# A fused retention and token-mixing kernel: q in rows of four tokens, one eviction for two products, other tiles for pairs 2 and 3, and a new order of all steps

## The chip, the cores and the metric

The kernel runs on one core of one Trainium2 chip. The metric is the device time of one execution in microseconds, on that core. PE is the matrix engine, DVE, ACT and POOL are the three engines that work on vectors, SP issues most of the transfers between HBM (DRAM) and SBUF; sixteen DMA engines carry them out.

## What is computed

The reference computes two layers one after the other, for 4 batches, 8 heads, 768 tokens and 64 values a head:

```python
for t in range(S):                       # layer 1, for each batch and head
    state = gamma * state + outer(k[t], v[t])
    y[t] = scale * q[t] @ state
x = y.transpose(0, 2, 1, 3).reshape(B, S, 512)
wq, wk = x @ w_q, x @ w_k                # layer 2: 512 -> 64 each
mixed = (scale2 * wq @ wk.T) @ x         # over the 768 tokens of a batch
out = relu(mixed) @ w_out                # 512 -> 512
```

gamma differs by head. q, k, v and the output are float32, 6.3 MB each.

## The kernel before, in words

The 768 tokens of a batch are cut into three *pairs* of two chunks of 128 tokens, twelve pairs in all (pair p is batch p // 3). The recurrence is done by chunks: within a chunk through a masked 128x128 product of k and q (scores), between chunks through the 64x64 state that PE accumulates in PSUM over the whole batch. The decay is split: v is multiplied by gamma to the power of minus t when it is cast (fv), y by gamma to the power of t when it is evicted (fy). The second layer uses that (wq wk^T) x = wq (wk^T x): PE accumulates z = wk^T x over a batch, and then multiplies wq by z, so nothing of the second layer behind z can start before a batch's last pair has its x.

Each pair passes through the same steps. Names of steps and tiles, with the lines of the profile:

- load (L151): q_st, k_st and v_st of 512 KB each, float32, two neighbouring tokens to a partition, so that the DRAM side is read in pieces of 512 B. Weights: L166 and L171.
- ck, cq, cv: cast to bf16 into ks, qs, vs (L136 on ACT, L137 on DVE and POOL; cv multiplies, L362 and L556).
- trk, trq: transposes on PE (L386, L585, L605); ekq, ek, eq evict them into kq (L136, L137).
- sc: scores (L417, L627); eat: mask and eviction into at_sb (DVE, L429, L639).
- st: state (L496, L678); es: its eviction into s_sb.
- in, ic, ia: the parts of y from the state (L461, L481, L664) and from the scores (L517, L698); ex: eviction with decay into x_nat (L530, L712).
- xt, exT: transpose of x (L730) and its eviction into xT; wqk: x @ w_k, and wq transposed (L749, L758); ew and ewt: their evictions into wk_n and wqT, two instructions.
- zm, ez: z and its eviction (L790); mx: wq times z (L809); r: relu (L824, L826); pj: the projection with w_out (L831), two of 512 columns for each pair; eo: eviction into o_st (L844, by L136 or L137).
- store (L860): 512 KB for a pair, or 256 KB for one half (s11/1).

TYPES says for each pair how its chunks lie: in type "2" a chunk lies on 64 partitions with two tokens each, and the matmuls on it are 64 rows deep; in type "1" the casts bring a chunk onto all 128 partitions (four casts of 64 x 512 for k, and four for v, in place of one of 128 x 1024), and scores, inner products and state take half as many matmuls.

The order of everything is written out by hand (or by a search done beforehand): ORDER is a list of steps with the engine (A, V, P) and the PSUM bank (@n), and each engine executes its steps in that order. fill.n are n matmuls on a zero tile whose result nobody reads. LOADS is the order on SP's queue: first all loads, then the stores s0, s1 and so on. SP takes one after the other: whatever waits holds up all that is behind it. STAGES = 18 staging buffers of 512 KB are reused as casts free them; OBUFS = 11 output buffers are reused as stores read them. The store's access pattern and the load's are these:

```python
dst = out[b, cp*2*C : (cp+1)*2*C, :].rearrange("(g j) m -> g j m", j=2)     # L856: 128 x 2 x 512
nc.sync.dma_start(out=dst, in_=src, max_dma_last_dim=OBYTES)                 # L860
```

Of the kernel before, what the change touches and what calls it, by code (L numbers as in the profile page):

```python
# [9 lines left out]
FP32 = mybir.dt.float32  # L10
# [6 lines left out]
ck.0.0:V ck.0.1:A fill.15@6 trk.0@0 cq.0.1:A cq.0.0:V fill.4@6 trq.0@0 cv.0.1:P cv.0.0:V ekq.0.1:A  # L17
ekq.0.0:A ck.1:A fill.6@6 st.0.0 cq.1:V cv.1:P cv.2:P es.0.0:A sc.0.1@0 cv.3:P eat.0.1:V mask:P
ck.4.0:P ck.2:A ck.4.1:P fill.2@6 st.0.1 cv.4.0:P sc.0.0@2 trq.1@4 cv.4.1:P trk.1@4 WO.1:P
ekq.1.1:V ekq.1.0:V es.0.1:V cq.2:A ck.5.0:P fill.1@6 ia.0.1@0 WO.0:P in.0@0 fill.2@6 sc.1.0@4  # L20
eat.0.0:V fill.4@6 sc.1.1@2 st.1.0 eat.1.0:V es.1.0:A ia.0.0@0 cv.5.0:P trk.2@4 ic.0@0 trq.2@4
st.1.1 eat.1.1:V ekq.2.0:V W:A cv.5.1:P ekq.2.1:A ex.0:V fill.3@6 sc.2.0@4 sc.2.1@2 in.1@0
eat.2.0:V ia.1.1@0 ia.1.0@0 es.1.1:A ck.6.1:P xt.0@4 st.2.0 cv.6.1:P eat.2.1:V ic.1@0 exT.0:V
ia.2.1@2 ex.1:V ia.2.0@2 ck.3:A es.2.0:A trk.3@4 ic.2@2 in.2@2 ex.2:V cv.6.0:P cv.7.0:P cq.3:A
wqk.0@6 trq.3@4 ekq.3.1:A ekq.3.0:V xt.1@0 st.3.0 exT.1:V es.3.0:A xt.2@2 cq.4:A exT.2:V cv.7.1:P
sc.3.0@4 ew.0:V sc.3.1@0 wqk.1@2 wqk.2@3 eat.3.1:V ewt.1:A ew.1:A trq.4@0 eat.3.0:V trk.4@0
ck.8.0:P ewt.2:A ew.2:A st.3.1 ic.3@2 cq.8:P cv.8.0:P cv.8.1:P in.3@2 ia.3.0@2 ia.3.1@2 ek.4:V
zm.0.0@4 ewt.0:V eq.4:A es.3.1:A ex.3:V cv.9.1:P sc.4.0@0 sc.4.1@5 st.4.0 eat.4.0:V xt.3@2 exT.3:V
eat.4.1:V es.4.0:A zm.0.1@4 ez.0:A mx.0@0 ck.5.1:A cq.5:V in.4.1@2 cv.9.0:P wqk.3@4 r.0:A ewt.3:A
ew.3:A ia.4.0@2 ia.4.1@2 in.4.0@2 trk.5@5 mx.1@0 ex.4:V st.4.1 trq.5@5 ek.5:V r.1:A eq.5:V  # L30
ck.10.1:P pj.0.1@4 eo.0.1:A pj.0.0@0 sc.5.0@5 es.4.1:V xt.4@3 sc.5.1@1 cv.10.0:P st.5.0 eo.0.0:A
pj.1.0@0 eat.5.0:V ck.6.0:A eat.5.1:V pj.1.1@5 exT.4:A es.5.0:V ia.5.0@3 ia.5.1@3 in.5.1@3
in.5.0@3 eo.1.0:A mx.2@0 eo.1.1:A ck.11.1:P cq.6:V ex.5:V wqk.4@2 ew.4:V trq.6@5 trk.6@5 eq.6:V
r.2:A xt.5@0 ek.6:V ewt.4:A pj.2.1@3 pj.2.0@2 sc.6.0@5 ck.7.1:A exT.5:V sc.6.1@0 wqk.5@4 eo.2.1:A
zm.1.0@3 cq.7:V eat.6.0:V ew.5:V eat.6.1:V st.6.0 zm.1.1@3 eo.2.0:A ck.7.0:A trk.7@5 es.6.0:A
trq.7@5 ez.1:A st.6.1 ewt.5:A eq.7:V ek.7:V mx.3@2 ia.6.1@0 ia.6.0@0 es.6.1:A st.7.0 r.3:A
in.6.1@0 es.7.0:A ex.6:V sc.7.0@5 mx.4@2 pj.3.1@4 r.4:A sc.7.1@0 eat.7.0:V pj.3.0@2 st.7.1 xt.6@5
eat.7.1:V exT.6:V ck.8.1:A eo.3.1:A pj.4.0@3 eo.3.0:A ia.7.1@1 es.7.1:A trq.8@5 cq.11:P in.7.0@1
ck.9.1:V trk.8@5 eo.4.0:A mx.5@3 in.7.1@1 eq.8:V ck.9.0:A ia.7.0@1 pj.4.1@0 r.5:A eo.4.1:A ek.8:V
sc.8.0@5 sc.8.1@3 cq.9:A st.8.0 ex.7:V es.8.0:A xt.7@1 exT.7:A pj.5.0@0 eat.8.1:V trq.9@3 trk.9@3  # L40
in.8.1@1 eo.5.0:A eat.8.0:V ek.9:V eq.9:A cv.10.1:P in.8.0@1 ia.8.1@1 cv.11.0:P ia.8.0@1 pj.5.1@0
ex.8:V wqk.6@6 xt.8@1 ew.6:V eo.5.1:A sc.9.1@3 cq.10:A exT.8:V wqk.7@0 wqk.8@1 ew.7:A zm.2.0@2
ck.10.0:A eat.9.1:V sc.9.0@3 ew.8:V ewt.6:A zm.2.1@2 st.9.0 ewt.8:A ez.2:A trk.10@5 trq.10@5
mx.6@1 eat.9.0:V es.9.0:A st.9.1 ewt.7:A in.9.1@3 r.6:A ek.10:V ia.9.0@3 ia.9.1@3 mx.7@0 eq.10:V
es.9.1:A ex.9:V ck.11.0:A r.7:A sc.10.0@5 eat.10.0:V st.10.0 pj.6.0@2 trk.11@3 trq.11@3 eq.11:V
ek.11:V eo.6.0:A sc.10.1@0 es.10.0:A xt.9@5 eat.10.1:V pj.6.1@2 in.10.0@3 cv.11.1:P in.10.1@3
exT.9:A sc.11.0@5 eo.6.1:A st.10.1 es.10.1:A eat.11.0:V wqk.9@2 ia.10.1@3 ia.10.0@3 ew.9:A ewt.9:A
sc.11.1@0 ex.10:V mx.8@5 eat.11.1:V st.11.0 r.8:A pj.7.1@2 in.11.0@3 xt.10@5 exT.10:V es.11.0:A
in.11.1@3 ia.11.0@3 ia.11.1@3 pj.8.0@0 ex.11:V wqk.10@1 eo.7.1:A xt.11@3 ewt.10:V exT.11:V ew.10:A
eo.8.0:A pj.7.0@6 wqk.11@3 ew.11:V eo.7.0:A zm.3.0@0 ewt.11:V zm.3.1@0 ez.3:A mx.11@0 r.11:A  # L50
mx.10@3 mx.9@5 pj.8.1@2 pj.11.1@0 eo.8.1:A pj.11.0@1 eo.11.1:A r.10:V r.9:A pj.10.0@2 pj.10.1@0
eo.10.0:A eo.11.0:V eo.10.1:A pj.9.1@6 eo.9.1:A pj.9.0@2 eo.9.0:A
# [4 lines left out]
q0 v0 k1 q1 v1 k2 q2 w v2 k3 q3 v3 k4 q4 v4 o0 o1 k5 q5 v5 k6 q6 v6 k7 q7 v7 k8 q8 v8 k9 q9 v9 k10  # L57
q10 v10 k11 q11 v11 s0 s1 s2 s3 s4 s5 s6 s7 s8 s11/1 s11/0 s10/0 s10/1 s9/1 s9/0
""".split()

TYPES = "222211111111"
STAGES = 18
OBUFS = 11
# [7 lines left out]
def kernel(  # L71
# [38 lines left out]
    stage_pool = pool("stage", STAGES)  # L110
# [33 lines left out]
    def load(name, p, half=None, eng=None):  # L144
        src = {"k": k, "q": q, "v": v}[name]
        b, cp = divmod(p, NP)
        st = pairs[p]
        if name + "_st" not in st:
            st[name + "_st"] = stage_pool.tile([128, 2, HP, 2, D], FP32, name=name + "_st", tag="st")
        xs = slice(0, 2) if half is None else slice(half, half + 1)  # L150
        dma = (eng or nc.sync).dma_start(  # L151
            out=st[name + "_st"][:, xs].rearrange("g x hp j d -> g (x hp) (j d)"),
            in_=src[b, xs.start * HP : xs.stop * HP, cp * 2 * C : (cp + 1) * 2 * C, :].rearrange(
                "h (g j) d -> g h (j d)", j=2
            ),
        )
    wstages = {}

    def load_weights(token):
        w_st = stage_pool.tile([128, 2, HP, 2, D], FP32, name=token + "_st", tag="st").rearrange(  # L160
            "p x hp j d -> p (x hp j d)"
        )
        if token == "w":
            st = w_st[:, 0 : 2 * NDM * DH].rearrange("p (w a h) -> p w a h", w=2, a=NDM)
            for i, src in enumerate((moe_w_q, moe_w_k)):
                nc.sync.dma_start(out=st[:, i], in_=src.rearrange("(a p) h -> p a h", p=128))  # L166
        else:
            st = w_st.rearrange("p (a m) -> p a m", a=2)
            for i in range(2):
                a = 2 * int(token[1:]) + i  # L170
                nc.sync.dma_start(  # L171
                    out=st[:, i], in_=moe_w_out[128 * a : 128 * a + 128, :], max_dma_last_dim=WBYTES
                )
        wstages[token] = st

    def load_token(token):
        if token[0] in "wo":
            load_weights(token)
        else:
            load(token[0], int(token[1:]))  # L180

    load("k", 0, 0, nc.scalar)
    load("k", 0, 1, nc.sync)

    queue = list(LOADS)
    staged = ["k0"]
    cast = set()

    def more_loads():
        while queue:
# [6 lines left out]
            n = len(staged)  # L199
            if n >= STAGES and staged[n - STAGES] not in cast:  # L200
                return
            staged.append(token)
# [4 lines left out]
    def release(token, n):  # L207
        parts[token] = parts.get(token, 0) + 1
        if parts[token] == n:
            cast.add(token)  # L210
# [25 lines left out]
    ty_b = const_pool.tile([128, NP * 2, H], FP32, name="ty_b")  # L236
    for t, base in ((ty, 0), (ty_b, 1 - C)):
        nc.gpsimd.iota(
            t,
            pattern=[[C, NP * 2], [0, H]],  # L240
            base=base,
            channel_multiplier=2,
            allow_small_or_imprecise_dtypes=True,
        )
    nc.gpsimd.tensor_copy(out=ty[64:128], in_=ty_b[64:128])
    fv = const_pool.tile([128, NP, H, 2], FP32, name="fv")
    fy = const_pool.tile([128, NP * 2, H], FP32, name="fy")
    nc.vector.tensor_tensor(out=tv, in0=tv, in1=ln_v, op=ALU.mult)
    nc.vector.tensor_tensor(out=ty, in0=ty, in1=ln_y, op=ALU.mult)
    nc.scalar.activation(out=fv, in_=tv, func=ACT.Exp)  # L250
    nc.scalar.activation(out=fy, in_=ty, func=ACT.Exp)

    fy1 = const_pool.tile([128, NP * 2, 2, HP], FP32, name="fy1")
    for cp in range(NP):
        nc.gpsimd.tensor_copy(
            out=fy1.rearrange("p (cp x) c hp -> p cp x c hp", x=2)[:, cp].rearrange("p x c hp -> p c x hp"),
            in_=fy[:, 2 * cp : 2 * cp + 2].rearrange("p c (x hp) -> p c x hp", x=2),
# [9 lines left out]
    def masks():  # L267

        for t, base in ((cmask, 0), (cmask_b, 128)):
            nc.gpsimd.memset(t, 1.0)  # L270
            nc.gpsimd.affine_select(
                out=t,
                in_=t,
                compare_op=ALU.is_ge,
                fill=0.0,
                base=base,
                pattern=[[-1, 2], [1, 2], [2, G]],
                channel_multiplier=-2,
            )
# [5 lines left out]
    cmask1 = const_pool.tile([128, 1, 2, G], BF16, name="cmask1")  # L285
    cmask1_b = const_pool.tile([128, 1, 2, G], BF16, name="cmask1_b")

    def masks1(e):

        for t, base in ((cmask1, 0), (cmask1_b, 127)):  # L290
            nc.gpsimd.memset(t, 1.0)
            nc.gpsimd.affine_select(
                out=t,
                in_=t,
                compare_op=ALU.is_ge,
                fill=0.0,
                base=base,
                pattern=[[0, 1], [1, 2], [2, G]],
                channel_multiplier=-2,
            )  # L300
        nc.gpsimd.tensor_copy(out=cmask1[64:128], in_=cmask1_b[64:128])

# [4 lines left out]
    def W(e):  # L307
        copy(
            e,
            wqk_sb[:, :, 0 : 2 * DH].rearrange("p a (r h) -> p a r h", r=2),  # L310
# [606 lines left out]
```

## Time and profile before

| | |
|---|---|
| time, median of 3 runs (lowest to highest) | 100.28 us (99.76 to 101.02) |
| span of the profiled execution, first to last instruction | 98.4 us |
| the profiled execution's own time | not listed |
| busy: PE, DVE, ACT, POOL | 85.4, 72.4, 64.4, 59.8 us |
| DMA | 26.74 MB, mean 272 GB/s |
| mean granted clock of PE | 0.965 |

The span is the profiler's, on the core; the time of a run has in it also what lies before the first and after the last instruction, so it is a little longer. The groups that take most of POOL are the casts of v (34.8 us, 32 of 1086 ns); of PE the projections (21.7 us) and the fills (11.0 us); of DVE the masked evictions of the scores (28.5 us, 24 of 1217 ns); of ACT the casts of k (13.6 us) and the evictions of the output (13.2 us). An engine's share of the span is an average over stages; the slices and windows further down show when each is full.

### The profile page before, as it was taken

To read this page: it belongs to the slowest core of one execution; us is meant where nothing else is said; L and a number is where in the kernel's file an instruction comes from. 1 tells how busy PE (TensorE), PEld (TensorE's weight loads), DVE (VectorE), ACT (ScalarE), POOL (GpSimd) and SP (SyncE) were. 2 spreads that over 40 slices of the span, in tenths; PEclk is the share of its full clock that TensorE was granted. 3 is DMA by queue.
4 is the path that set the end of the run, shared out by engine and by line. 5 is a ranking of instruction groups with operands and counts; after the bars stand their busy time and mean duration, and the time that the engine had idled before them with its cause. 6 is when DMAs were issued, how large, how long until landed. Compare 5 with 4: busy or idle time off the path is not lost. (4 is left out here: it accounts for less than half of the span.)

```text
span 98.4 us, 4214 instructions
## 1 busy us (share of the span) xinstructions
PE 85.4 (87%) x1847; PEld 54.9 (56%) x1861; DVE 72.4 (74%) x105; ACT 64.4 (65%) x110; POOL 59.8 (61%) x77
## 2 busy tenths in 40 slices
PE   4999789876697988999999999689999999989950
PEld 1334465564585775655747647357786576644410
DVE  3032489999489299979999899998899999624200
ACT  4344823928090458969799899987899955347750
POOL 4646070250989998999999999999999800000000
PEclk9999999999955699999999999999999999999999
DMA  1999998999999999999999999999998150040983
GB/s 18 291 347 347 339 343 200 308 295 309 314 335 316 301 271 286 333 320 316 315 330 318 272 307 295 336 327 341 394 401 321 37 214 9 0 191 22 388 340 125
DMA packets 43954, 26.74 MB, mean 272 GB/s; under 512 B 1952, under 2 KB 40864, under 8 KB 43936
## 3 DMA queue, kind: packets, MB, share of 16 engines
q1 hardware_dynamic: 43408, 26.22, 86.1%
q8 instruction: 14, 0.23, 0.9%
q10 hardware_dynamic: 528, 0.26, 0.9%
q14 instruction: 4, 0.03, 0.1%
HBM read 20.19 MB, written 6.29 MB: 269 GB/s over the span
## 5 line engine op out<-in xcount | busy, mean ns | idle before, releaser
L556 POOL TENSOR_TENSOR vs<-v_st,fv 64x512 bf16<-64x512 f32 x32 | 34.8, 1086 | 2.2 <-DMA v_st<-in_v_dram 0.2
L831 PE MATMUL banks<-wout_sb,relu 128*128 128x512 bf16 x85 | 21.7, 380 | 1.0 <-issue 0.6
L639 DVE TENSOR_TENSOR at_sb<-banks,cmask 128x1024 bf16<-128x1024 f32 x16 | 19.1, 1217 | 1.1 <-PE banks L627 1.1
L136 ACT CAST ks<-k_st 64x512 bf16<-64x512 f32 (+2 forms) x20 | 13.6, 682 | 5.9 <-DMA k_st<-in_k_dram 5.6
L362 POOL TENSOR_TENSOR vs<-v_st,fv 128x1024 bf16<-128x1024 f32 (+1 forms) x4 | 7.2, 1810 | 13.2 <-DMA v_st<-in_v_dram 13.2
L136 ACT COPY o_st<-banks 128x512 f32<-128x512 f32 x23 | 13.2, 587 | 2.7 <-PE banks L831 2.5
L137 DVE COPY kq<-banks 128x1024 bf16<-128x1024 bf16 x18 | 11.8, 686 | 2.5 <-PE banks L585 1.8
L831 PEld LDWEIGHTS <-relu 128*128 128x128 bf16 x96 | 8.2, 98 | 8.8 <-issue 0.4
L824 ACT ACTIVATE relu<-banks 128x1024 bf16<-128x1024 f32 x11 | 11.3, 1024 | 2.1 <-PE banks L809 1.6
L328 PE MATMUL banks<-warm 128*128 128x512 bf16 x34 | 11.0, 467 | 1.6 <-DVE warm L218 1.3
L136 ACT COPY kq<-banks 128x1024 bf16<-128x1024 bf16 x6 | 6.0, 1011 | 6.5 <-PE banks L386 4.6
L712 DVE TENSOR_TENSOR x_nat<-banks,fy 128x1024 bf16<-128x1024 f32 x8 | 9.8, 1220 | 0.6 <-PE banks L664 0.3
L429 DVE TENSOR_TENSOR at_sb<-banks,cmask 128x1024 bf16<-128x1024 f32 x8 | 9.4, 1216 | 0.4 <-PE banks L417 0.2
L137 POOL CAST ks<-k_st 64x512 bf16<-64x512 f32 x14 | 8.5, 608 | 0.8
L758 PE MATMUL banks<-xT,wqk_w 128*128 128x256 bf16 x48 | 8.1, 297 | 0.0
L136 ACT CAST qs<-q_st 128x1024 bf16<-128x1024 f32 (+1 forms) x6 | 5.9, 979 | 2.9 <-DMA q_st<-in_q_dram 2.9
L136 ACT CAST s_sb<-banks 128x256 bf16<-128x256 f32 x17 | 6.4, 377 | 1.2 <-PE banks L678 1.0
L328 PEld LDWEIGHTS <-warm 128*128 128x128 bf16 x37 | 3.7, 114 | 6.1 <-issue 3.2
L627 PE MATMUL banks<-kq 64*128 64x128 bf16 x128 | 5.9, 217 | 1.1 <-DVE kq L137 0.8
L137 DVE CAST qs<-q_st 128x1024 bf16<-128x1024 f32 (+1 forms) x5 | 4.2, 850 | 3.3 <-DMA q_st<-in_q_dram 3.3
L137 DVE COPY xT<-banks 128x1024 bf16<-128x1024 bf16 x9 | 6.2, 685 | 0.3 <-PE banks L730 0.3
L530 DVE TENSOR_TENSOR x_nat<-banks,fy 128x1024 bf16<-128x1024 f32 x4 | 4.9, 1218 | 1.7 <-PE banks L461 1.6
(78 smaller groups left out, 134.6 us busy)
## 6 DMA issues: line engine op xcount, KB each, us to landing
q_st<-in_q_dram SPq DMA_DIRECT2D x12, 512.0 KB, 6.6
v_st<-in_v_dram SPq DMA_DIRECT2D x12, 512.0 KB, 6.5
k_st<-in_k_dram SPq DMA_DIRECT2D x11, 512.0 KB, 6.4
out_dram<-o_st SPq DMA_DIRECT2D x9, 512.0 KB, 6.4
out_dram<-o_st SPq DMA_DIRECT2D x6, 256.0 KB, 2.0
o_st<-in_moe_w_out_dram SPq DMA_DIRECT2D x4, 256.0 KB, 5.2
k_st<-in_k_dram ACTq DMA_DIRECT2D x1, 256.0 KB, 4.2
k_st<-in_k_dram SPq DMA_DIRECT2D x1, 256.0 KB, 3.9
```

What stands on the lines that cost most here:

```text
L136: return nc.scalar.copy(out=out, in_=in_)
L137: return ENGINES[e].tensor_copy(out=out, in_=in_)
L328: nc.tensor.matmul(out=bank32(b), lhsT=warm[:, 0:128], rhs=warm, start=True, stop=True)
L362: ENGINES[e].tensor_tensor(out=st["vs"][:, :, :, xs].rearrange("p hp j x d -> p x (hp j) d"), in0=st["v_st"][:, xs].rearrange("p x hp j d ...
L429: ENGINES[e].tensor_tensor(out=st["at", half].rearrange("p x hi j t -> p (x hi) (j t)"), in0=st["at_ps", half].rearrange("p (n t) -> p n t ...
L556: ENGINES[e].tensor_tensor(out=st["vs"][rows(j), c].rearrange("p hp x d -> p x hp d"), in0=st["v_st"][rows(c), :, :, j], in1=fv[rows(c), p ...
L627: nc.tensor.matmul(out=ps[:, x, hi, c, :], lhsT=st["kT"][rows(x), hp, c, :], rhs=st["qT"][rows(x), hp, c, :], start=(hi == 0 and c == 0), ...
L639: ENGINES[e].tensor_tensor(out=st["at", half].rearrange("p x hi c t -> p (x hi c) t"), in0=st["at_ps", half].rearrange("p (n t) -> p n t", ...
L712: nc.vector.tensor_tensor(out=st["x"].rearrange("p x c i n -> p (x c i n)").rearrange("p (m d) -> p m d", d=D), in0=st["y_ps"].rearrange(" ...
L758: nc.tensor.matmul(out=st["wq_ps"], lhsT=wqk_sb[:, a, 0 : 2 * DH], rhs=st["xT"][:, a].rearrange("p c t -> p (c t)"), start=False, stop=(a ...
L824: nc.scalar.activation(out=dst, in_=st["mx_ps"], func=ACT.Relu)
L831: nc.tensor.matmul(out=bank32(b), lhsT=st["relu"][:, a, j, :], rhs=wout_sb[:, a, :], start=(a == 0), stop=(a == NDM - 1),)
```

## The change

q is loaded with four neighbouring tokens to a partition (pieces of 1024 B): the first four heads go to partitions 0 to 63, the others to 64 to 127, by two transfers for each pair. The tokens of a chunk therefore come out of the transposes in another order, the masks and the decay fy are made for that order, and the store writes rows in it: for each half y, two groups of 64 partitions, rows of 2048 B. Heads 2n and 2n+1 now share a tile (before: n and n+4). Pairs 2 and 3 go from type "2" to the form that was "1" and is now "R". Some transposes are done with all 128 rows at once (":f"). wk and wq of a pair are evicted by one instruction of 384 columns (ew) in place of two (ew, ewt). zm is issued pair by pair. Staging is in 7 slots of three pairs of one tensor, output buffers are 9. ORDER and LOADS are new throughout: more steps of POOL (casts of k and q) and more output evictions on DVE, the small fills spread over the first pairs. The diff's core:

```diff
 LOADS = """
-q0 v0 k1 q1 v1 k2 q2 w v2 k3 q3 v3 k4 q4 v4 o0 o1 k5 q5 v5 k6 q6 v6 k7 q7 v7 k8 q8 v8 k9 q9 v9 k10
-q10 v10 k11 q11 v11 s0 s1 s2 s3 s4 s5 s6 s7 s8 s11/1 s11/0 s10/0 s10/1 s9/1 s9/0
+q0 v0 k1 q1 k2 v1 q2 k3 v2 q3 w v3 k4 k5 q4 v4 q5 v5 o0 o1 k6 q6 v6 k7 q7 v7 q8 k8 v8 k9 q9 v9 q11 k11 k10
+q10 v10 v11 s2 s8 s1 s4 s5 s6 s3 s0 s7 s11/1 s11/0 s9/1 s9/0 s10/1 s10/0
 """.split()
-TYPES = "222211111111"
-STAGES = 18
-OBUFS = 11
+TYPES = "22RRRRRRRRRR"
+SLOTS = 7
+OBUFS = 9
...
+        if name == "q":
...
+            for i in range(2):
+                nc.sync.dma_start(
+                    out=st["q_st"][rows(i)].rearrange("g hi x j d -> g (hi x) (j d)"),
+                    in_=q[p // NP, i * HP : i * HP + HP, p % NP * 2 * C : (p % NP + 1) * 2 * C, :].rearrange(
+                        "h (g j) d -> g h (j d)", j=4
+                    ),
+                )
+            return
...
     def ew(e, b, p):
         st = pairs[p]
-        st["wk"] = moe_pool.tile([128, 2, DH], BF16, name="wk_n")
-        copy(e, st["wk"], st["wk_ps"])
-
-    def ewt(e, b, p):
-        st = pairs[p]
-        st["wqT"] = moe_pool.tile([128, 2, 2, G], BF16, name="wqT")
-        copy(
-            e,
-            st["wqT"].rearrange("p j c g -> p c j g"),
-            st["wq_ps"].rearrange("p (c j g) -> p c j g", c=2, j=2),
-        )
+        wkq = moe_pool.tile([128, 6, G], BF16, name="wkq")
+        copy(e, wkq.rearrange("p n g -> p (n g)"), st["w_ps"])
...
     def xt(e, b, p):
         st = pairs[p]
+        if e == "f":
+            ps = half_banks(b, 0).rearrange("p c (a t) -> p c a t", a=NDM)
+            for c in range(2):
+                for a in range(NDM):
+                    nc.tensor.transpose(ps[:, c, a], st["x"][:, c, a // 2, a % 2, :], identity)
...
     def stored(name):
...
-        dst = out[b, cp * 2 * C : (cp + 1) * 2 * C, :].rearrange("(g j) m -> g j m", j=2)
+        dst = out[b, cp * 2 * C : (cp + 1) * 2 * C, :].rearrange("(g jj y) m -> jj g y m", jj=2, y=2)
         src = pairs[p]["o"]
-        if j:
-            dst, src = dst[:, int(j)], src[:, int(j)]
-        nc.sync.dma_start(out=dst, in_=src, max_dma_last_dim=OBYTES)
+        for y in js:
+            nc.sync.dma_start(out=dst[:, :, y], in_=src[:, y], max_dma_last_dim=OBYTES)
         return True
```

As instructions, each load of q is 64 x 4 x 256 elements (it was 128 x 8 x 128), and each store has 2 x 64 x 512 on the DRAM side and 128 x 512 in SBUF (it was 128 x 2 x 512 or 128 x 512 on both). In the new file the projections are L929 and the store is L957. The first and last lines of the new ORDER, and two from where the second half begins its last pairs:

```diff
+cq.0.1:P ck.0.1:A fill.15@6 ck.0.0:A trk.0@0 cq.0.0:A cv.0.0:P cv.0.1:V fill.3@6 trq.0@0 ekq.0.0:A st.0.0
+fill.3@6 es.0.0:A st.0.1 ekq.0.1:V sc.0.1@0 sc.0.0@2 fill.2@6 eat.0.1:V ia.0.1@0 cq.1:A trq.1@4 mask:P
...
+pj.8.0@4 eo.8.0:A mx.6@0 sc.10.0@2 r.6:A cv.10.0:P st.10.0 es.10.0:A pj.8.1@4 eat.10.0:V eo.8.1:A cv.10.1:P
...
+cv.11.0:P ia.10.1@0 st.11.0 es.11.0:A in.10.0@0 in.10.1@0 ex.10:V mx.7@2 in.11.0@4 in.11.1@4 cv.11.1:P
+ia.11.0@4 ia.11.1@4 ex.11:V wqk.9@6 ew.9:V r.7:A pj.7.0@0 xt.10@1 exT.10:V xt.11@3 exT.11:V pj.6.0@5
+eo.6.0:V wqk.10@1 wqk.11@2 zm.3.0@3 ew.10:V zm.3.1@3 ew.11:A zm.3.2@3 ez.3:A mx.11@1 r.11:A eo.7.0:V mx.9@3
+mx.10@5 pj.7.1@0 eo.7.1:V r.9:A pj.11.1@1 pj.11.0@2 eo.11.0:A eo.11.1:V pj.9.1@0 pj.9.0@1 r.10:V eo.9.0:V
+pj.10.1@2 eo.10.1:V eo.9.1:A pj.10.0@0 eo.10.0:A
```

## The prediction

> **What bounds the kernel now.** First I read the slices of the span for PE, POOL and the DMA engines.
>
> ```profile
> PE   4999789876697988999999999689999999989950
> POOL 4646070250989998999999999999999800000000
> PEclk9999999999955699999999999999999999999999
> DMA  1999998999999999999999999999998150040983
> GB/s 18 291 347 347 339 343 200 308 295 309 314 335 316 301 271 286 333 320 316 315 330 318 272 307 295 336 327 341 394 401 321 37 214 9 0 191 22 388 340 125
> ```
>
> A slice is 2.46 us. The DMA engines are full from 2.5 to about 76 us, POOL from 27 to 79, PE from 35 to 95 (with a half-speed clock just before). Three resources are full one beside the other; what each has left after the others decides the end. The windows give that in numbers (columns: PE, weight loads, DVE, ACT, POOL busy, clock, DMA share, GB/s).
>
> ```profile
> 25.00:30.00 5.00, 4.49 (x128) 3.64 (x128) 3.60 (x6) 2.29 (x3) 4.61 (x9) 0.67 1.12 325
> 30.00:35.00 5.00, 4.47 (x117) 3.55 (x118) 3.17 (x4) 1.31 (x5) 4.67 (x6) 0.64 1.05 308
> 35.00:65.00 30.00, 27.39 (x594) 17.86 (x599) 28.88 (x35) 25.82 (x45) 28.14 (x30) 1.00 1.05 309
> ...
> 70.00:75.00 5.00, 4.84 (x127) 3.69 (x125) 4.46 (x6) 4.93 (x12) 4.66 (x6) 1.00 1.05 403
> 75.00:80.00 5.00, 4.87 (x122) 3.36 (x122) 4.77 (x6) 4.33 (x9) 3.39 (x4) 1.00 0.31 111
> 80.00:85.00 5.00, 4.90 (x107) 3.17 (x106) 4.56 (x6) 2.00 (x4) 0.00 (x0) 1.00 0.21 77
> ...
> 93.00:93.50 0.50, 0.50 (x4) 0.20 (x2) 0.00 (x0) 0.43 (x1) 0.00 (x0) 1.00 1.04 397
> ```
>
> The stores cost almost nothing: after 76 us the DMA engines are mostly idle, and a burst of stores runs at 397 GB/s. PE alone sets the end, as the end of the chain of waits shows.
>
> ```profile
> 88.77 6.00 PE banks L831 x27
> 94.77 0.02 issue
> 94.80 0.59 ACT o_st L136
> ```
>
> Then the DMA view and the issues of loads and stores.
>
> ```profile
> DMA packets 43954, 26.74 MB, mean 272 GB/s; under 512 B 1952, under 2 KB 40864, under 8 KB 43936
> L151 SPq DMA_DIRECT2D v_st<-in_v_dram x12: 574/1398/2605, 1.8 to 62.4; - x12
> out_dram<-o_st SPq DMA_DIRECT2D x6, 256.0 KB, 2.0
> ```
>
> Of the 1952 short packets 1024 are the 256-byte rows of the two small weights (2 x 128 x 4). The other 928 are 58 transfers x 16: each transfer is dealt in 16 shares, one for each DMA engine, and ends with one short packet on each. All 58 have 128 rows outermost on both sides. The last load is issued at 62.4 and lands 6.5 later (the median), 68.9. A store of 256 KB lands 2.0 after its issue; 262144 B at 397 GB/s are 0.66 of these, so 1.3 us are fixed.
>
> The span is 98.4 and the profiled execution's own time is not listed; against the median of 100.28, 1.9 us lie around the span. About 2% is what a measurement can tell from no change: 98.3 to 102.3.
>
> **The change, part by part.**
>
> *Stores.* Before: nine of 512 KB and six of 256 KB, 128 rows outermost. After: 24 of 256 KB, each with 2 x 64 rows of 2048 B on the DRAM side (two row groups outermost, then 64 rows), 128 rows on the SBUF side. No row shows a transfer whose outermost count is below 16. If the dealing goes by the outermost counts, two groups give two shares, and two of 16 engines do all the work. An engine's rate is 397/16 = 24.8 GB/s, so a store takes 262144/49.6e3 = 5.28 us instead of 0.66. If the pair of engines is the same each time, 24 stores follow one another: 24 x 5.28 = 126.8 us. Bounds: 24 x 0.66 = 15.8 us, hidden beside PE as now, if dealing is by 16; 24 x 5.42 = 130 at the 388 GB/s of the third slice from the end, 24 x 5.20 = 124.9 at the 403 of 70 to 75 us. I take 126.8, because every transfer that the trace shows in 16 shares has an outermost count that 16 divides, and this one has 2. The Trainium skill, "DMA: Bandwidth & Descriptors", section "Why a DMA increments its semaphore by 16 and not by 1", says that a transfer uses the largest number of engines up to 16 that divides the slowest dimension of both access patterns, always the lowest-numbered ones. By that rule it is two, the same two each time; the 928 short packets agree for 128 rows, and no run here shows a smaller count. At the 27.2 GB/s that the skill's "SBUF — State Buffer" gives for one port, the 24 stores would be 116 us, an estimate.
>
> *Loads of q.* Twelve of 512 KB (128 rows, 512-byte pieces) become 24 of 256 KB (64 rows, 1024-byte pieces). Twelve more issues on SP, at the 0.42 to 0.57 of its first three unhindered ones, are 6 us of SP, hidden: a pair's two issues take 1.0 and its bytes 1.7 (512 KB at 309 GB/s). If SP fell behind, these 6 us would be added to the loads. Bytes: longer pieces can bring q to the 397 GB/s of the 2 KB rows, 1.32 instead of 1.70, -4.5 us over twelve; if half of the partitions means half of the width, 3.4, +20.4 us. No row is near; I take the middle, +8. The Trainium skill, "SBUF — State Buffer", section "Door 1: The DMA port swizzle", has 196 GB/s for partitions 0 to 63 and 328 for all 128, and only 6% from a second transfer to the other half. By that a q pair is 2.7 us, +12 over twelve, an estimate: the sum would be 4 us higher; no run here shows a 64-row transfer. The stores stand behind all loads on SP. So the engines come to them at 68.9 - 1.3 + 8 = 75.6 (63.1 to 88.0).
>
> *One eviction for wk and wq.* Twelve instructions fewer. Before: six of 0.283 and three of 0.417 on DVE, six of 0.271 and nine of 0.379 on ACT, 8.0 us. After: seven on ACT and five on DVE of 384 columns, about 0.49 and 0.55 by the step from 128 to 256 columns: 6.2. The 1.8 us lie on engines with 26 and 34 us idle: nothing; in the last pair's chain the later of two becomes one longer, +0.2.
>
> *Pairs 2 and 3 on 128 rows* (TYPES changes both). PE per pair by the lines' busy time: scores 0.92 to 0.74, inner products 0.73 to 0.66, state 0.82 to 0.50, inter and cross 0.67 to 0.44: -0.8 a pair, -1.6 in all. The casts split: v from 1.9 to four of 1.086 on POOL, k from 1.05 to four of 0.61. With the steps that change engine POOL has 38 of 1.086, 18 of 0.608, five of q and the rest: 61 against 55 us, +6.7; ACT +4; DVE -1.5. POOL had 13.2 us of waiting for v before 25 us to take it up, and is full after that; at worst its last cast is 6.7 later than 78.6.
>
> *Shared tiles of neighbouring heads.* The same instructions with other strides: ACT's cast took 617 ns for 64 rows in 2x4x64 and 618 for 128 rows in 8x64, DVE's x_nat 1218 and 1220 in two orders. Nothing.
>
> *Full transposes* in five steps (8 of 128x128 for 16 of 64x64) and 35 fills for 37: 16 take 0.41 us, 8 about the same; -0.4 for the fills.
>
> *Orders.* Stores go s2, s8, s1, s4, s5, s6, s3, s0, s7, 11, 9, 10. In SP's queue s8 waits for eo.8.1, and six pairs that are done long before wait behind it. With nine output buffers where there were eleven, pair 9 takes the buffer of pair 0: eo.9.0 on DVE waits for s0, the 15th and 16th store, and behind it stand eo.10.1 and, through the banks, the last projections. In the slow-store case s0 ends at 75.6 + 16 x 5.28 = 160, and s7 and s11 (four stores, 21 us) cover these few evictions.
>
> **Sum.** With stores on two engines nothing but the loads' end counts: compute is done, but for pairs 9 and 10, at about 100, beside the stores. 75.6 + 126.8 + 1.3 fixed = 203.7 of span, + 1.9 = 205.6; I say 205. Its own range: 63.1 + 124.9 + 3.2 = 191 to 88.0 + 130 + 3.2 = 221; I keep 188 to 218, a little lower since two engines that run alone may each be faster than a sixteenth.
>
> **Rivals.**
>
> *1. Stores on 16 engines, data decides.* For it: 16 shares in all 58 transfers. The last v lands at 68.9 + 8 = 76.9, its casts (4 x 1.086) end at 81.3, or at up to 85.3 by POOL's extra work. From there by rows: inner 0.65, x_nat 1.22, transpose 0.41, xT 0.69, wqk 0.67, eviction 0.5, zm 0.29, z 0.38, mx 0.28, relu 1.02, six projections of 0.87, eviction 0.59, and 3.0 from the last eviction to the end as now: 14.9. That ends at 96.2 to 100.2, a time of 98 to 102: no difference. With loads at +12 to +20, v lands at 81 to 89 and the time is 102 to 110: slower.
>
> *2. Faster: the clock.* Before, the granted clock is 0.67 and 0.64 from 25 to 35 us: 0.33 x 5 + 0.36 x 5 = 3.4 us of matmul time lost; PE is full from 35 to the end, so what is gained there comes out at the end. The new order spreads small fills between the first pairs. If the clock holds, 100.3 - 3.4 = 97. It decides only if stores go by 16 and v11 lands no later than about 75.
>
> *3. Two engines, but another two for each store.* Then stores overlap and only the last one's 5.28 against 0.66 shows: 100 + 4.6 = 105. Against it: all stores come from one queue in the same form.
>
> **Chances.** Stores on one pair of engines 0.62. On 16 engines: no difference 0.17, slower through late loads 0.10, faster by the clock 0.07. Alternating pairs 0.04. So faster 0.07, same 0.17, slower 0.76. The likeliest alone has 188 to 218; eight in ten need part of the case of no difference as well: 98 to 216, which leaves out the faster case and the ends.
>
> **What would show it.** Right: stores of 256 KB that land over 5 us after the one before, a DMA share near 2/16 = 0.12 and about 50 GB/s for more than 100 us after the last load; short packets 1024 + 55 x 16 + 24 x 2 = 1952 (by 16 shares 2288); SP waits on landings, not on evictions. Wrong: stores that land after 2 us and a chain that ends in L929. For q: landings past 7 us and a rate under 309 GB/s mean the half width. For rival 2: PEclk without the dip at 27 to 34 us (slices 12 to 14).

## The result, and the profile after

201.38 us, median of 4 runs (200.58 to 201.45), against 100.07 (99.76 to 101.02) on the same chip: a ratio of 2.007, interval 1.992 to 2.022. The profiled execution took 201.4, its span is 199.7; 1.7 lie around it. The executions of one kernel scatter by up to 4.5%; each ratio and interval here compares only those near the kernel's fastest, so it need not be the quotient of the two medians, and where too few were near it, a time stands without an interval.

The slices of the span of the changed kernel, as above; one slice is now 4.99 us.

```profile
PE   7777768889969988998900000000000000000000
POOL 5664699987599839920000000000000000000000
PEclk9999969999999999999965555555555555555555
DMA  5999999999999992111111111111111111111110
GB/s 163 307 309 302 241 292 269 309 280 276 222 268 245 283 273 94 55 55 51 51 51 51 51 53 51 51 51 51 51 51 51 51 51 51 51 51 51 51 51 37
```

PE has nothing left to do from slice 21 on, at 100 us, and POOL from slice 19 on. From there to the end data still moves, but the DMA line stands at 1 tenth. The windows give the share in hundredths (columns as in the prediction).

```profile
25.00:30.00 5.00, 3.54 (x56) 3.02 (x58) 2.31 (x4) 4.68 (x9) 4.73 (x5) 0.66 1.00 291
...
35.00:65.00 30.00, 26.14 (x565) 17.47 (x569) 26.39 (x31) 24.55 (x37) 25.16 (x26) 1.00 1.09 266
...
75.00:80.00 5.00, 4.27 (x107) 3.00 (x107) 3.64 (x6) 3.28 (x6) 4.73 (x6) 1.00 0.27 89
80.00:85.00 5.00, 4.95 (x94) 3.01 (x93) 4.86 (x5) 4.79 (x8) 4.68 (x6) 1.00 0.14 54
...
110.00:130.00 20.00, 0.00 (x0) 0.00 (x0) 0.00 (x0) 0.00 (x0) 0.00 (x0) 0.50 0.13 52
```

0.13 is two engines of sixteen (0.125), and 51 to 52 GB/s are 25.6 for each. The loads end near 75.7 us: in the window from 75 to 80, 89 GB/s x 5 us are 445 KB, of which the stores at 51 take 255; the other 190 KB are 0.7 us at the 271 GB/s of the window before (an estimate; the rate falls over two microseconds). From there 24 stores fill (199.7 - 1.3 - 75.7) = 122.7 us, 5.11 us each.

The DMA line, the issues of the stores on SP, and the two evictions that waited for a store:

```profile
DMA packets 37809, 26.73 MB, mean 134 GB/s; under 512 B 1952, under 2 KB 34720, under 8 KB 37792
```

```profile
L957 SPq DMA_DIRECT2D out_dram<-o_st x24: 506/4949/7106, 71.2 to 180.2; - x24
```

```profile
83.62 4.40 SPq L957
88.06 18.46 DMA out_dram<-o_st
106.65 0.69 DVE o_st L134
```

1952 short packets: 1024 small rows, 55 transfers with 16 shares and 24 with two. The kernel before has 1952 too, by chance: 58 x 16 is 55 x 16 + 24 x 2. So the count speaks only against the 2288 that 16 shares for each store would have given. An issue of a store took 0.5 us where nothing was in its way and 4.9 at the median: SP comes to stand behind the stores, and nothing but stores is left on it. The last store was issued at 180.2 and the DMA engines stop at 198.3, so three or four stores stand in the queue at a time, and still only two engines work. The last three lines are the end of the chain of waits: the last eviction (pair 10) waits for a buffer until 106.6, and even that ends 92 us before the last store.

### The profile page after: what moved, and what is told of

Its sections match the earlier page's. It is cut to its first block, busy times and chain, and to the rows that moved or that the text cites. A ratio compares the mean times of both kernels' runs of the same rounds, so it can differ in the third digit from the quotient of the medians.

```text
span 199.7 us, 3978 instructions
## 1 busy us (share of the span) xinstructions
PE 84.5 (42%) x1702; PEld 54.4 (27%) x1719; DVE 73.1 (37%) x106; ACT 68.9 (34%) x104; POOL 65.8 (33%) x87
## 2 busy tenths in 40 slices
DMA packets 37809, 26.73 MB, mean 134 GB/s; under 512 B 1952, under 2 KB 34720, under 8 KB 37792
## 3 DMA queue, kind: packets, MB, share of 16 engines
HBM read 20.19 MB, written 6.29 MB: 133 GB/s over the span
## 4 chain that ended last, share of the span: by engine, by line
DMA 19%; SPq 18%; POOL 6%; ACT 4%; PE 4%; issue 3%; DVE 0%; ACTq 0%; DVEq 0%
DMA out_dram<-o_st 9%; SPq L167 9%; DMA q_st<-in_q_dram 6%; SPq L175 5%; POOL vs L650 5%; DMA v_st<-in_v_dram 3%; SPq L957 2%; PE banks L929 1%; ACT ks L133 1%; SPq L200 1%; ACT o_st L133 1%; PE banks L791 1%; POOL ks L134 1%; ACT qs L133 1%; PE banks L673 1%
## 5 line engine op out<-in xcount | busy, mean ns | idle before, releaser
L650 POOL TENSOR_TENSOR vs<-v_st,fv 64x512 bf16<-64x512 f32 x38 | 40.9, 1077 | 6.1 <-PE banks L791 2.0
L732 DVE TENSOR_TENSOR at_sb<-banks,cmaskr 128x1024 bf16<-128x1024 f32 x20 | 23.9, 1218 | 1.0 <-issue 0.6
L929 PE MATMUL banks<-wout_sb,relu 128*128 128x512 bf16 x84 | 22.8, 380 | 0.7 <-issue 0.2
L133 ACT CAST ks<-k_st 64x512 bf16<-64x512 f32 (+1 forms) x24 | 14.8, 616 | 3.8 <-DMA k_st<-in_k_dram 3.5
L134 POOL CAST ks<-k_st 64x512 bf16<-64x512 f32 (+1 forms) x19 | 12.0, 634 | 7.5 <-DMA k_st<-in_k_dram 6.7
L133 ACT COPY kq<-banks 128x1024 bf16<-128x1024 bf16 x12 | 12.0, 1015 | 4.0 <-PE banks L460 2.5
L134 DVE COPY o_st<-banks 128x512 f32<-128x512 f32 x9 | 6.2, 687 | 12.1 <-DMA out_dram<-o_st 8.2
L929 PEld LDWEIGHTS <-relu 128*128 128x128 bf16 x96 | 8.1, 97 | 8.6 <-issue 0.6
L791 PE MATMUL banks<-vs,at_sb 128*128 128x64 bf16 x160 | 7.4, 196 | 0.0
L791 PEld LDWEIGHTS <-at_sb 128*128 128x128 bf16 x160 | 6.2, 100 | 2.0 <-issue 0.4
L771 PE MATMUL banks<-vs,ks 128*64 128x64 bf16 x128 | 5.1, 203 | 1.3 <-POOL vs L650 0.7
L506 DVE TENSOR_TENSOR at_sb<-banks,cmask 128x1024 bf16<-128x1024 f32 x4 | 4.8, 1220 | 2.1 <-PE banks L494 2.1
```

Source lines behind the costliest of these rows:

```text
L133: return nc.scalar.copy(out=out, in_=in_)
L134: return ENGINES[e].tensor_copy(out=out, in_=in_)
L650: ENGINES[e].tensor_tensor(out=tokens_st(p, "v")[rows(j), c].rearrange("p hp x d -> p (hp x) d"), in0=pair_st(p, "v")[rows(c), :, j], in1= ...
L732: ENGINES[e].tensor_tensor(out=st["at", half].rearrange("p x hi c t -> p (x hi c) t"), in0=st["at_ps", half].rearrange("p (n t) -> p n t", ...
L791: nc.tensor.matmul(out=y[:, x, c, hp, :], lhsT=st["at", half][:, x, hi, c, :], rhs=st["vs"][:, c, hp, x, :], start=first1(p, x), stop=Fals ...
L929: nc.tensor.matmul(out=bank32(b), lhsT=st["relu"][:, a, j, :], rhs=wout_sb[:, a, :], start=(a == 0), stop=(a == NDM - 1),)
```

## The experiments

A word on the names: those with b_ are edits of the kernel before, those with a_ of the changed one. Each ratio is to the kernel before, timed beside it.

**How many engines a store gets: b_store2, b_store4, b_store16.** The kernel before, with its 24 stores of 256 KB in a shape of 2, 4 or 16 groups of rows outermost on the DRAM side. Nothing else is changed. The diff is that of b_store2, as 24 stores in two groups.

```diff
-        dst = out[b, cp * 2 * C : (cp + 1) * 2 * C, :].rearrange("(g j) m -> g j m", j=2)
+        dst = out[b, cp * 2 * C : (cp + 1) * 2 * C, :].rearrange("(g a y) m -> a g y m", a=2, y=2)
...
+        for y in js:
+            nc.sync.dma_start(out=dst[:, :, y], in_=src[:, y], max_dma_last_dim=OBYTES)
```

> The kernel before with nothing changed but its stores: 24 of 256 KB with 2 x 64 rows outermost on the DRAM side (the rows land in another order than the reference's). If the store alone explains the result: loads leave the engines at about 67.6, then 24 x 5.1 us, 1.3 to land, 1.9 around the span: 193 to 196. If the other parts of the change have a share in it: clearly less, 150 or below.

> The same with 4 x 32 rows outermost. If the number of engines is the outermost count: 102 GB/s, 2.56 us a store, 67.6 + 61.4 + 3.2 = 132. If an outermost count below 16 always means two engines or the permuted rows are the cause: 195 as with 2. If two is a special case: 100.

> The same with 16 x 8 rows outermost, the control for the row order and for 24 stores in place of 15. Outermost count: all 16 engines, 99 to 102, as before. Scattered rows or the number of stores as the cause: near 195.

Measured: 195.01 (ratio 1.953, 1.932 to 1.975), 134.03 (1.343, 1.326 to 1.360) and 102.83 (1.030, 1.023 to 1.037). The windows late in each, and the issues of the stores:

```profile
100.00:130.00 30.00, 0.00 (x0) 0.00 (x0) 0.00 (x0) 0.00 (x0) 0.00 (x0) 0.51 0.13 51
```

```profile
100.00:130.00 30.00, 0.00 (x0) 0.00 (x0) 0.00 (x0) 0.00 (x0) 0.00 (x0) 0.50 0.26 100
```

```profile
L859 SPq DMA_DIRECT2D out_dram<-o_st x24: 1252/4948/7155, 64.3 to 171.1; - x24
```

```profile
L859 SPq DMA_DIRECT2D out_dram<-o_st x24: 796/2386/4446, 64.1 to 115.5; - x24
```

```profile
L859 SPq DMA_DIRECT2D out_dram<-o_st x24: 538/553/1417, 62.5 to 97.0; - x24
```

The first of each kind is b_store2, the next b_store4, the last line b_store16. Two groups: a share of 0.13, 51 GB/s, 4.95 us for an issue at the median. Four: 0.26, 100 GB/s, 2.39 us. Sixteen: 0.55 us, the issues are hardly held up. The short packets count with it: 1760, 1808 and 2096, that is 1024 + 43 x 16 + 24 x 2, 4 or 16. So this one edit, with nothing else of the change, nearly doubles the time of the kernel before, and the count of the outermost dimension says by how much. The Trainium skill, "DMA: Bandwidth & Descriptors", section "Why a DMA increments its semaphore by 16 and not by 1", has this rule, and these three runs agree with it. b_store16 is 3% over, a little more than expected: its stores land after 3.7 us at the median (before 2.0), and the mean clock of its profile is 0.949 (before 0.965). Of the 2.7 us by which its profiled span is longer (101.1 against 98.4), 1.6 lie ahead of the last eviction, which starts at 96.38 in place of 94.80, and 1.1 behind it, with the last store. That the clock makes the first part is not shown.

**The stores repaired in the changed kernel: a_rows64, a_rows128, a_st.** Three ways to give the stores their engines back. a_rows64 writes the same rows by two transfers of 64 partitions each. a_rows128 writes 128 rows outermost as before, from columns of mx that lie two apart for it. (The edit exchanges y and jj of the changed store's pattern, so a partition does not hold two neighbouring tokens as the expectation says, and half of the rows land elsewhere; the number and sizes of all instructions and transfers are as meant.) a_st takes the store of before and leaves mx alone. The diff is that of a_rows64:

```diff
-            nc.sync.dma_start(out=dst[:, :, y], in_=src[:, y], max_dma_last_dim=OBYTES)
+            for jj in range(2):
+                nc.sync.dma_start(out=dst[jj, :, y], in_=src[rows(jj), y], max_dma_last_dim=OBYTES)
```

> The changed kernel with each store of 2 x 64 rows issued as two stores of 64 rows; same bytes, rows and order, 48 stores of 128 KB. If the outermost count 2 confines a store to two of 16 engines, 64 rows are dealt over 16 again, the stores hide beside PE as before, and the end is PE's: the last projections ended at 99.5 us, so a span of about 101 to 104 and a time of 103 to 106. If instead the scattered rows (2 KB in steps of 8 KB) or the number of stores make them slow, it stays near 200.

> The changed kernel, but mx writes its columns so that a partition again holds two neighbouring tokens, and the stores are those of before (128 rows outermost, nine of 512 KB and six of 256 KB). The stores with 64 rows moved 205 GB/s. If the stores' form is all that costs (count of engines with 2 x 64 rows, half the width with 64), the stores hide again beside PE, the last projection ends near 99.5 as in both runs of the change, and the time is 99.5 + 3 + 1.9 = 104. If the change is slow for another reason behind the loads as well, it stays above 107.

> The changed kernel with the stores in the form of before (128 rows outermost, nine of 512 KB and six of 256 KB) and nothing else changed; each partition's row goes to another place than the reference's. mx is as in the change, so its 48 matmuls need 0.22 us for four and not the 0.43 that a_rows128 needed with columns two apart: 2.5 us of PE less. If the loads of q are what is left: last load issued near 69 as in a_rows128, the last projection ends at 97 to 99 and the time is 101 to 103.

Measured: a_rows64 115.73 (1.159, 1.148 to 1.169), ten over what was expected; a_rows128 105.37 (1.057, 1.023 to 1.090); a_st 105.06 (1.044, 1.031 to 1.057), two over. a_rows64 late, and its stores:

```profile
95.00:100.00 5.00, 4.40 (x21) 1.78 (x19) 3.30 (x4) 2.08 (x4) 0.00 (x0) 1.00 0.89 206
100.00:105.00 5.00, 0.00 (x0) 0.00 (x0) 0.00 (x0) 0.02 (x1) 0.00 (x0) 0.81 0.88 205
```

```profile
L958 SPq DMA_DIRECT2D out_dram<-o_st x48: 466/595/2850, 71.3 to 110.9; - x48
```

Here all engines work (0.88) but move 205 GB/s, where the stores of before ran at 397 in a burst: a transfer that reads 64 of the 128 partitions has about half the rate. SP's issues, 0.595 us for 128 KB, would alone allow 220 GB/s, close to what was measured. But the packet records of the trace tell the two apart: a piece of 2048 B took 147 ns at the median in a_rows64, and 84 in the kernel before, in b_store2 and in b_store16. So the transfers themselves are slow. SP waits for the eviction of s8 until about 83 us; the 42 stores behind it are 5.5 MB, 26.9 us at 205, and as only some 170 GB/s were reached from 85 to 95, the span is 114.1. Splitting the store by partitions is thus no repair. a_rows128 and a_st are, for the stores: they end with PE, as before. In a_rows128 the columns of mx lie 8 bytes apart in PSUM, and its matmuls take half as long again (first line a_rows128, second the changed kernel):

```profile
L907 PE MATMUL banks<-wkq,z_sb 64*128 64x256 bf16 x48 | 6.9, 403 | 0.5 <-ACT z_sb L133 0.5
```

```profile
L907 PE MATMUL banks<-wkq,z_sb 64*128 64x256 bf16 x48 | 4.4, 272 | 1.0 <-DVE at_sb L732 0.5 <-ACT z_sb L133 0.5
```

The 2.5 us don't show in the time (105.37 against 105.06), within what these runs tell apart.

So with the stores repaired the changed kernel is still slower than before, by some 4 to 6%. The rest was sought in the loads of q.

**The loads of q by themselves: b_q64, b_q128, b_q64_1k, b_q64_two.** All in the kernel before. b_q64 loads q by two transfers of 64 partitions with pieces of 512 B; b_q128 by two transfers of 128 partitions with four heads each; b_q64_1k as the changed kernel does, 64 partitions with pieces of 1024 B; b_q64_two as b_q64, with the upper half on ACT's queue. The diff is that of b_q64:

```diff
+        if name == "q":
+            for i in range(2):
+                nc.sync.dma_start(
+                    out=st["q_st"][rows(i)].rearrange("g x hp j d -> g (x hp) (j d)"),
+                    in_=src[b, :, cp * 2 * C + i * C : cp * 2 * C + i * C + C, :].rearrange(
+                        "h (g j) d -> g h (j d)", j=2
+                    ),
+                )
+            return
```

> The kernel before, each load of q cut into two of 64 rows (512-byte pieces as before). If 64 rows mean half the width (205 GB/s as the 64-row stores): a q pair takes 2.56 in place of 1.70 us, the last load is issued 10 us later than 62.4, near 72, and the time is 100 to 104. If the width does not matter: last issue 62 to 64 and a time of 99.5 to 100.5.

> The kernel before, each load of q cut into two of 128 rows and four heads, the control for the number and size of the transfers. If the number of transfers is what costs (twelve more issues, eight in flight): last issue late as with 64 rows. If the width is: last issue 62 to 64, a time of 99.5 to 101.

> The same with pieces of 1024 bytes, the form of the changed kernel (values go to other places in the tile, so that the result is not the reference's). If longer pieces make up for the half width: last issue at 62 to 65. If not: as with 512-byte pieces, near 72.

> The kernel before with each load of q in two halves of 64 rows, the lower one on SP's queue, the upper one on ACT's. If a half is slow because 64 rows reach half of the width and the two stand behind each other in one queue, both halves now run beside each other and the rate of 5 to 15 us goes back from 308 towards 343 GB/s. If a 64-row transfer is slow by itself (or the queues take turns): it stays near 308. The time says little, since ACT waits at its issues.

Measured: b_q64 104.48 (1.044, 1.025 to 1.064), b_q128 101.16 (1.013, 0.999 to 1.027), b_q64_1k 105.65 (104.00 to 106.98) with no interval, b_q64_two 132.83 (1.322, 1.296 to 1.347). b_q64 and b_q128 are each half a microsecond or less over what was expected. The windows from 35 to 65 us of b_q64 and b_q128, where the DMA engines do nothing but load (before: 309 GB/s):

```profile
35.00:65.00 30.00, 27.30 (x636) 18.29 (x638) 25.00 (x33) 22.98 (x42) 23.96 (x27) 0.98 1.07 259
```

```profile
35.00:65.00 30.00, 27.22 (x625) 17.95 (x622) 28.63 (x35) 25.08 (x43) 28.40 (x29) 1.00 1.04 305
```

The DMA share is full in both, so it can't tell them apart; only the last column can. Twelve more transfers cost next to nothing (305), and 64 partitions cost a sixth of the whole stream (259). If q is a third of the bytes and k and v still go at 309, q's own rate is r in 1/259 = (2/3)/309 + (1/3)/r: 196 GB/s, an estimate. By it q's 6.29 MB take 32.1 us instead of 20.4, 11.7 more; the last load was issued at 73.6 instead of 62.4. With pieces of 1024 B the rate of this window is 275 GB/s in b_q64_1k, whose last load is issued at 68.7, between the two values that were expected. The same loads in the changed kernel, in a_st, go at 276:

```profile
35.00:65.00 30.00, 26.83 (x575) 17.60 (x573) 26.44 (x30) 23.91 (x36) 26.11 (x28) 1.00 1.15 276
```

The same equation gives q 227 GB/s there, an estimate, 7.3 us more over the whole; the last load was issued at 69.9, 7.5 later. Longer pieces win back about a third of the loss. Two queues do not: from 5 to 15 us b_q64_two moved 309 GB/s and b_q64 308, the kernel before 343; its time is likely ACT's, which spends the first 18.9 us on its issues (five of them take 17.57 us) and does no other work meanwhile. The Trainium skill, "SBUF — State Buffer", section "Door 1: The DMA port swizzle", has 196 GB/s for partitions 0 to 63; the 205 of a_rows64 and the estimate of 196 agree. In the section "Can I just issue two DMAs to hit both halves?" the same page of the Trainium skill has 6% from a second transfer to the other half; the 309 against 308 GB/s of the two queues agree in that next to nothing is won.

**What is left when both transfers are as before: a_st_q and a_best.** a_st_q is a_st with q loaded by one transfer of 128 partitions. a_best puts the casts, transposes and masks of q in the order for it as well: the changed kernel without its two new transfers. Of a_best's diff only the lines of the two transfers stand here; without the lines taken out, q goes through the load that k and v use.

```diff
-            for i in range(2):
-                nc.sync.dma_start(
-                    out=st["q_st"][rows(i)].rearrange("g hi x j d -> g (hi x) (j d)"),
...
-        dst = out[b, cp * 2 * C : (cp + 1) * 2 * C, :].rearrange("(g jj y) m -> jj g y m", jj=2, y=2)
+        dst = out[b, cp * 2 * C : (cp + 1) * 2 * C, :].rearrange("(g j) m -> g j m", j=2)
```

> The same and q loaded as before, one transfer of 128 rows for each pair (its tokens land in other places, so values differ). If half the width of q's loads is the rest of the loss: last load issued at 61 to 64 and a time of 97 to 100. If POOL's 6.7 us more work, the new order or the two pairs on 128 rows cost too: 101 to 104 though the loads are early.

> The changed kernel with both transfers in the form of before: q by one load of 128 rows with two tokens to a partition (its casts, transposes and masks in that order too), the stores with 128 rows outermost. Kept of the change: one eviction for wk and wq, pairs 2 and 3 on 128 rows, tiles shared by neighbouring heads, the new orders. Theory (all of the loss lies in the form of the two transfers; what is left is a small gain, from the clock that no longer dips before 35 us): 97.5 to 99.5 us, a ratio of 0.97 to 0.99 to the kernel before, last load issued at 62 to 63, granted clock about 0.99. Rival (the gain of the run with misplaced q came from its own data flow, or from noise): 100 to 102, ratio at 1.0 or over. Rival (the dip comes back with the other transposes and fills of q): a clock near 0.965 and 100 to 101.

Measured: a_st_q 98.67 (97.61 to 99.38), the kernel before beside it 101.26 (99.78 to 102.21), no interval. Its last load is issued at 62.9, and its time is in the range of the first case, so with the loads on time POOL's added work does not show as a loss. a_best 98.49, six runs from 96.82 to 99.73, before 101.58: a ratio of 0.974, interval 0.963 to 0.985, faster than both kernels. Its clock by slices, three windows, and the end of its chain of waits:

```profile
PEclk9999999999999999999999999999999999999998
```

```profile
25.00:30.00 5.00, 4.24 (x108) 3.22 (x107) 4.67 (x7) 4.06 (x7) 4.63 (x6) 1.00 1.05 304
30.00:35.00 5.00, 4.24 (x124) 3.36 (x116) 3.74 (x6) 4.24 (x6) 4.30 (x5) 1.00 1.09 325
35.00:65.00 30.00, 29.15 (x654) 18.99 (x648) 28.57 (x34) 28.26 (x42) 27.89 (x30) 1.00 1.06 313
```

```profile
84.83 6.16 PE banks L890 x28
91.02 0.58 ACT o_st L133
```

The loads are back at 313 GB/s, and the clock is 1.00 from 25 to 35 us where it had been 0.67 and 0.64. The last eviction starts at 91.0; it was 94.8. The two profiled spans differ by 98.4 - 95.1 = 3.3 us, the prediction's price for the clock was 3.4. That fits, but the cause is not shown. This profile is of the fastest of a_best's six executions, whose spans are 95.1 to 98.0. And at like mean clocks, 0.975 to 0.983, three of them span 96.8 to 98.0 us and eleven executions of the kernel before 97.7 to 100.2: the medians, 98.0 and 98.8, differ by 0.8 us that the clock does not explain. The merged eviction, pairs 2 and 3, the tiles and the order were not tried one by one, so what each of them gives stays open.

The three sizes put together: stores 201.38 - 105.06 = 96.3; loads of q 105.06 - 98.67 = 6.4 (between 5 and 9, from the lowest and highest times of the two); the rest 0.026 x 101.6 = 2.6 the other way. Their sum is 100.1; the change measured 201.38 - 100.07 = 101.3 (the runs are of several chips).

## Why the prediction was right, and where it was not

- *Two engines for each store, the same two.* Right, and shown: b_store2 makes nearly all of the loss alone, and the share of 0.13 never goes beyond two engines. The short packets are the 1952 foretold. Rival 3 (pairs that alternate) would have let stores overlap; with three or four in the queue, the flat 51 GB/s excludes it.
- *A store at 5.28 us.* Mis-sized by 3%: 5.11. An engine moved 25.6 GB/s, not the 24.8 of a sixteenth of a burst. 24 x 0.17 = 4.1 us, which is the whole of what 205 was too much (3.6). (At 388 GB/s the bound is 5.41, not 5.42, which changes nothing.) By the 27.2 GB/s for one port in the Trainium skill, "SBUF — State Buffer", section "Door 1: The DMA port swizzle", the stores would take 116 us, an estimate; 122.7 were measured.
- *The loads of q at +8, so 75.6.* Right in size: 75.7. This is in part luck, as 8 was the middle of two cases and no row stood behind it. The cause is the half width (b_q64, b_q128), softened by the longer pieces (b_q64_1k, a_st).
- *Twelve more issues on SP hidden.* Right within 1.5 us: b_q128 has them, and its last load was issued at 63.9 in place of 62.4.
- *One eviction of 384 columns at 0.49 on ACT, 0.55 on DVE.* The groups measure 484 ns on ACT (7) and 552 on DVE (5). That it is worth nothing was not tried by itself.
- *POOL's last cast up to 6.7 later than 78.6.* 7.4: the last eight casts began at 77.19 and took 8.82, to 86.0. a_best has as many casts and ends them at 77.0, so it is not POOL's work that is late but its data. The prediction charged this lateness to POOL's added work, at 6.7; the work measured 6.0 (65.8 us busy against 59.8).
- *Pair 9 takes the buffer of pair 0 and waits for s0 until 160.* Wrong in place and size: pair 10 waited, to 106.6. Buffers pass on in the order in which the stores are issued, s2, s8, s1, and the wait was for s1, the sixth store: 75.7 + 6 x 5.11 = 106.4. The prediction had taken buffers by the number of the pair. It cost nothing, as the stores behind it covered it.
- *s8 blocks SP's queue.* So it did: SP issued its second half at 83.6, right behind the eviction of 82.46. It was hidden here by s2, and in a_rows64 it cost time. The waits that the profile names for SP at the stores are on evictions (8.1 us in two); the stand behind landings shows only in the long issues.
- *Rival 1 (the stores by 16): 98 to 102, no difference.* The case with repaired stores is a_st: 105.06. The step that failed is the tail at +8: the casts were taken to end at 81.3 to 85.3 and the rest to need 14.9. They ended at 85.7. In the new order the casts of v10 and v11 stand in a row on POOL, eight and not four (in a_best too, from 68.23 to 77.04), and in a_st they stood behind the cast of q10, which waited for its load until 74.55. The rest took 17.2. With +8 on the loads the answer was slower, the other half of that rival.
- *Rival 2 (the clock): 97.* In a_best's profile the dip is gone: a mean clock of 0.997 and 96.82 us; over its six executions the clock was 0.977 to 0.997 and the median 98.49. What brings the dip is open: a_st, with the loads of q late, has 1.00 from 25 to 35 us too, and 0.84 from 5 to 15. In the changed kernel itself one window keeps 0.66 (25 to 30 us), 0.34 x 5 = 1.7 us in place of 3.4, hidden by the stores.

## What to carry to other kernels

Look at the outermost count of both access patterns of each transfer before anything else: with two row groups outside, a store got two of sixteen DMA engines here, and no saving in the load's pieces pays for that. A full DMA share says nothing of the rate: transfers over 64 of 128 partitions kept all engines busy at half to three quarters of the speed (205 GB/s against 397 for the stores, some 227 against 309 for the loads), so read the last column of the windows. And when a change of many parts loses, put its parts back one at a time: here everything but the two transfers was worth 2.6%.

## What was not expected of the hardware

- Splitting a transfer in two by partitions did not use both halves one beside the other: 48 stores of 64 partitions from one queue ran at 205 GB/s, with 147 ns for a piece of 2048 B in place of 84; and with the loads of q split, the stream ran at 309 from two queues as at 308 from one.
- Pieces of 1024 B in place of 512 brought loads of 64 partitions from some 196 to 227 GB/s (both estimates from the windows).
- mx with its columns 8 bytes apart in PSUM: 403 ns in place of 272 for a matmul of 256 columns, in one run.
